# Attention products of a float32 kernel as 64 x 64 x 64 matmuls on the four quarters of the array, scores and outputs in one pair of PSUM banks

## The chip, the cores and the metric

The kernel runs on one core of a Trainium2 chip. A core has five engines with queues of their own: TensorE (PE in the profile; its weight loads are PEld), VectorE (DVE), ScalarE (ACT), GpSimd (POOL) and SyncE (SP, which here only issues transfers). The metric is the device time of one execution in microseconds (us).

## The reference

Chunked softmax attention, then two feed-forward layers, all in float32. Batch 8, 8 heads, 576 tokens, head size 64, chunks of 64 tokens; 4608 tokens in all, width 512, inner width 2048:

```python
scores = q_c @ k_c.T / sqrt(64)            # per batch, head and chunk: 64 x 64
attn = exp(scores - max(scores)); attn = attn / (sum(attn) + 1e-9)
x = attn @ v_c                             # 64 x 64, then heads side by side: [4608, 512]
h = x @ w_in1;  g = max(h, 0) + alpha * min(h, 0);  x = g @ w_out1
h = x @ w_in2;  out = (h - tanh(h)) @ w_out2
```

The layers' weights are float64 and are rounded to float32 on the chip.

## The kernel before

**The large products.** A layer runs over nine blocks of 512 tokens, layer 1 first and then layer 2. A block has 16 steps, one for each 128 inner features f: `up` (L414) makes `hps`, 128 features by 512 tokens, with 12 matmuls; `act_g` and `split_g` put it through the activation and split it into a high and a low part (`ghi`, `glo`); `down` (L472) adds it to the four accumulators `y` with 12 more matmuls, two steps later (`LAG`). Each of these 24 matmuls has 128 rows, 128 columns of weights and 512 moving columns.

**The attention beside it.** Tokens 0 to 511 (tiles 0 to 3, 128 tokens each, which are two chunks) have their attention worked out before the loop by functions with `_early` in their names. The 32 later tiles are worked out inside the blocks of layer 1, one block ahead of their use. A tile t goes through these stages, each put on a step of the plan by `at(step, ...)`, `s = base[t]` being its first:

- `att_a` (DVE transposes of 32 x 32 blocks) or `att_a_natural` (tiles 4 to 8 and three later ones: PE transposes `tr`, evicted by DVE and ACT) makes `qt` (queries, features on partitions) and `kbd`. In `kbd` the keys of the two heads of a pair stand block-diagonally, with zeros between, so that one matmul with 128 rows serves both heads.
- `att_s` (step s): 8 matmuls, one per head pair and chunk, 64 weight columns (`qt`) and 128 moving columns (`kbd`), into the bank `sc`.
- `att_e` (s+1) and `att_n` (s+2): maximum `mx`, difference, exponential `p`, sum `sm`, reciprocal `rd`, product on POOL.
- `att_t`, `att_d` (s+3): DVE transposes `p` into `pt`; four DVE and four ACT copies bring the 32 x 32 blocks into `ptb`, block-diagonal by chunk, zeros between.
- `att_v` (s+5): 8 matmuls, one per head, 64 weight columns (`v`) and 128 moving columns (`ptb`), into the bank `xp`.
- `att_x` (s+6): ACT and DVE split `xp` into `xh` and `xl`, which the next block's `up` reads.

Each of these matmuls is plain float32 and stands in the trace as two instructions. In steady state the tiles' first steps are four apart.

**What sets the order.** A scheduler orders each engine's instructions by the plan and by its own forecast of when operands are ready. An engine then takes its instructions in that order. While block 0 runs (to about 160 us), DVE, ACT and POOL also round the first layer's weights to float32 (`wm`, `w`; L107 to L154), and each `up` and `down` of that block waits for its own piece.

PSUM has eight banks: two for `hps`, four for `y`, one for `sc`, one for `xp`.

Of the kernel before, what the change touches and what calls it, by code (L numbers as in the profile page):

```python
# [18 lines left out]
# (h - tanh(h)) / h**3 = CC (s + CA) ((s + CB)**2 + CE), s = h*h, to float32 accuracy where |h| < 3/8  # L19
# [8 lines left out]
def kernel(  # L28
# [49 lines left out]
    kbd = const.tile([P, 2, HP, 2, 2, D], F32, name="kbd")  # L78
    ptb = const.tile([P, H, 2, D], F32, name="ptb")

# [157 lines left out]

    def att_a_natural(t):
        if t not in qts:  # L240
            new_qt([t, t + 1] if t in (4, 6) else [t])
        raw = raws.pop(t)
        for i in range(2):
            tr = ps_a.tile([P, HP, P], F32, tag=("sc", "xp")[i], name="tr")
            for hp in range(HP):
                nc.tensor.transpose(tr[:, hp, :], raw[i][:, hp * P:(hp + 1) * P], ident)
            if i == 0:
                nc.vector.tensor_copy(qts[t].rearrange("p h c d -> p h (c d)"), tr)
            else:
                for e in range(2):  # L250
                    r = slice(64 * e, 64 * e + 64)
                    nc.scalar.activation(
                        out=kbd[r, t % 2, :, :, e, :], in_=tr[r].rearrange("p h (c d) -> p h c d", c=2), func=AF.Copy
                    )
# [11 lines left out]
    def att_a(t):  # L266
        if t not in qts:
            new_qt((t, t + 1))
        raw = raws.pop(t)
        nc.vector.transpose(  # L270
            out=qts[t].rearrange("p h c d -> p h (c d)"), in_=raw[:, 0].rearrange("p h g i -> p h (g i)")
        )
        for e in range(2):
            r = slice(64 * e, 64 * e + 64)
# [5 lines left out]
    scs = {}  # L280

    def att_s(t, tag="sc"):
        qt = qts.pop(t)
        sc = ps_a.tile([P, HP, 2, D], F32, tag=tag, name="sc")
        for hp in range(HP):
            for c in range(2):
                nc.tensor.matmul(  # L287
                    out=sc[64 * c:64 * c + 64, hp],
                    lhsT=qt[:, hp, c, :],
                    rhs=kbd[:, t % 2, hp, c],  # L290
                    start=True,
                    stop=True,
                )
        scs[t] = sc

    def att_s_early(t):
        qt, kt = qts.pop(t), kts.pop(t)
        sc = ps_a.tile([P, HP, 2, D], F32, tag=("sc", "xp")[t % 2], name="sc")
# [13 lines left out]
    def att_e(t, early=False):  # L312
        scv = scs.pop(t).rearrange("p a e d -> p (a e) d")
        mx = stat.tile([P, H, 1], F32, tag="mx", name="mx")
        nc.vector.tensor_reduce(out=mx[:, :, 0], in_=scv, op=ALU.max, axis=AX.X)
        pool, tag = (stage, "st") if early else (att, "p")
        p = pool.tile([P, H, D], F32, tag=tag, name="p")
        nc.vector.tensor_tensor(out=p, in0=scv, in1=mx.to_broadcast([P, H, D]), op=ALU.subtract)
# [18 lines left out]
    def att_d(t):  # L337
        """Each 32 x 32 block goes to the partitions of its keys; the result is block-diagonal by chunk."""
        pt = pts.pop(t)
        for c in range(2):  # L340
            for a in range(2):
                o, i = 64 * c + 32 * a, 64 * c + 32 * (1 - a)
                nc.vector.tensor_copy(ptb[o:o + 32, :, c, 32 - 32 * a:64 - 32 * a], pt[i:i + 32, :, a, :])
                nc.scalar.activation(
                    out=ptb[o:o + 32, :, c, 32 * a:32 * a + 32], in_=pt[o:o + 32, :, a, :], func=AF.Copy
                )

    def att_v(t):
        vt = vts.pop(t)
        xp = ps_a.tile([P, HP, P], F32, tag="xp", name="xp")  # L350
        for hp in range(HP):
            for e in range(2):
                nc.tensor.matmul(  # L353
                    out=xp[64 * e:64 * e + 64, hp],
                    lhsT=vt[:, 2 * hp + e],
                    rhs=ptb[:, 2 * hp + e].rearrange("p c d -> p (c d)"),
                    start=True,
                    stop=True,
                )
# [27 lines left out]
    def x_parts(t, o):  # L387
        return ((xps[t], o, P),) if t >= NPT else ((xps[t][0], o, D), (xps[t][1], o + D, D))

    def att_xh(t, x, o):  # L390
        for xp, u, n in x_parts(t, o):
            nc.scalar.activation(out=x[0][:, :, u:u + n], in_=xp, func=AF.Copy)

    def att_xl(t, x, o):
        for xp, u, n in x_parts(t, o):
            nc.vector.tensor_tensor(  # L396
                out=x[1][:, :, u:u + n], in0=xp, in1=x[0][:, :, u:u + n].bitcast(F32), op=ALU.subtract
            )
# [48 lines left out]
    def tanhshrink(g, hp, n, f):  # L447
        """h - tanh(h); where |h| < 3/8 as h^3 times a cubic in h^2 that is the quotient to
        float32's accuracy, since the difference would cancel."""
# [7 lines left out]
        mask = kbd.bitcast(U32).rearrange("p u h c e d -> p (u h c e d)")[:, f % 2 * n:(f % 2 + 1) * n]  # L457
# [82 lines left out]
    turn = {4: 2, 5: 2, 6: 6, 7: 6, 8: 11}  # L540
    free = 0
    for unit in units:
# [15 lines left out]
        for t in unit:  # L558
            s = base[t]
            if t in turn:  # L560
                at(turn[t], att_a_natural, t)
# [35 lines left out]
    with tc.manual_schedule():  # L597
        make_identity(nc, ident)
        nc.vector.memset(zero, 0.0)
        nc.vector.memset(kbd, 0.0)  # L600
        nc.vector.memset(bias_sb, TS[1])
        nc.gpsimd.memset(ptb, 0.0)
# [171 lines left out]
```

## Time and profile before

| | |
|---|---|
| three runs | 1745.61, 1746.21, 1746.31 us; median 1746.21 |
| the profiled execution, first to last instruction | 1745.2 us |
| TensorE's mean granted clock there | 0.992 of full |
| busy: PE, DVE, ACT, POOL | 98%, 77%, 40%, 20% |
| layer 1 beyond block 0, 200 to 840 us | PE busy all 640 us, DVE 455 us |

Busy time is the union of an engine's instructions. Matmuls overlap in the pipeline, so that what a group of them costs is read from the distance between the starts of the groups around it, not from its own busy time.

### The profile page before, as it was taken

The page shows a single profiled execution, that of the slowest core. Times are in us where ns is not written, and L with a number is a line of the kernel's source. Part 1 is how long each engine was busy: PE and PEld are TensorE (multiplying, and loading weights), DVE is VectorE, ACT ScalarE, POOL GpSimd, SP SyncE. Part 2 cuts the span into 40 slices and gives each one's busy share as a digit, 9 for nine tenths or more (in the row PEclk, how much of TensorE's full clock was granted, in tenths as well). Part 3 has the DMA queues.
Part 4 walks back from the last instruction along what each step waited for, and adds up shares of the span by engine and source line. Part 5 has one row for each costly group of instructions (what it writes and reads, how often), then busy time and mean ns, then how long its engine had stood idle before and what let it go on. Part 6 is the DMA issues. An engine that isn't in the chain of part 4 may idle for free.

```text
span 1745.2 us, 22786 instructions
## 1 busy us (share of the span) xinstructions
PE 1704.2 (98%) x8365; PEld 1379.3 (79%) x8365; DVE 1344.3 (77%) x2188; ACT 694.5 (40%) x1312; POOL 345.4 (20%) x265
## 2 busy tenths in 40 slices
PE   8889999999999999999999999999999999999997
PEld 7667887888878888788888778788888888888885
DVE  8999857877677868675436787878788888888776
ACT  6665323323332324232334453434343434444433
POOL 2555000000000000000243222222222222222221
PEclk9999999999999999999999999999999999999999
DMA  9912306332252513320332010101010101000000
GB/s 248 259 50 55 109 14 144 80 101 75 76 113 42 152 31 127 61 79 7 127 91 73 1 48 1 48 1 49 1 48 1 49 1 49 1 25 1 24 1 25
DMA packets 215583, 108.45 MB, mean 62 GB/s; under 512 B 170912, under 2 KB 187312, under 8 KB 215472
## 3 DMA queue, kind: packets, MB, share of 16 engines
q1 hardware_dynamic: 215472, 107.01, 22.3%
q8 instruction: 65, 1.06, 0.3%
q14 instruction: 46, 0.38, 0.1%
HBM read 79.70 MB, written 27.26 MB: 61 GB/s over the span
## 4 chain that ended last, share of the span: by engine, by line
PE 61%; DVE 25%; ACT 8%; issue 5%; DMA 0%; SPq 0%; ACTq 0%; DVEq 0%
PE y L472 29%; PE hps L414 28%; DVE g L461 4%; DVE g L463 4%; DVE g L462 4%; DVE g L459 3%; ACT sq L454 2%; ACT ghi L444 2%; ACT w L456 2%; PE xp L353 2%; PE sc L287 2%; DVE kbd L458 2%; ACT th L455 1%; DVE xl L503 1%; DVE g L431 1%
## 5 line engine op out<-in xcount | busy, mean ns | idle before, releaser
L414 PE MATMUL hps<-xh,w 128*128 128x512 f32 (+1 forms) x2312 | 592.5, 396 | 11.5 <-ACT w L153 7.9
L414 PEld LDWEIGHTS hps<-xh,w 128*128 128x128 f32 x2312 | 430.2, 190 | 114.8 <-ACT w L153 8.8
L444 ACT ACTIVATE ghi<-g 128x512 fp32r<-128x512 f32 x288 | 181.9, 632 | 761.3 <-DVE g L463 450.1
L445 POOL TENSOR_TENSOR glo<-g,ghi 128x512 fp32r<-128x512 f32 x159 | 214.9, 1351 | 622.3 <-ACT ghi L444 580.2
L414 PE MATMUL hps<-xl,w 128*128 128x512 f32 (+1 forms) x1156 | 308.7, 389 | 0.0
L472 PE MATMUL y<-w,ghi 128*128 128x512 f32 x1152 | 294.0, 393 | 9.8 <-ACT ghi L444 5.2
L472 PE MATMUL y<-ghi,w 128*128 128x512 f32 x1152 | 292.3, 394 | 5.0 <-ACT ghi L444 2.5
L472 PEld LDWEIGHTS y<-w,ghi 128*128 128x128 f32 x1152 | 214.6, 188 | 62.4 <-ACT ghi L444 11.1
L472 PEld LDWEIGHTS y<-ghi,w 128*128 128x128 f32 x1152 | 217.3, 190 | 53.0 <-ACT ghi L444 3.5
L414 PEld LDWEIGHTS hps<-xl,w 128*128 128x128 f32 x1156 | 217.0, 188 | 45.3 <-DVE xl L396 0.3
L458 DVE TENSOR_SCALAR kbd<-sq 128x512 uint32<-128x512 f32 x144 | 136.5, 948 | 136.2 <-ACT sq L454 136.2
L435 DVE TENSOR_SCALAR g<-hps,alpha_sb 128x512 f32<-128x512 f32 x128 | 95.5, 746 | 113.6 <-PE hps L414 112.0
L329 POOL TENSOR_TENSOR p<-p,rd 128x512 f32<-128x512 f32 x35 | 38.2, 1091 | 632.2 <-DVE rd L328 554.6
L472 PE MATMUL y<-w,glo 128*128 128x512 f32 x576 | 159.6, 390 | 0.0
L472 PE MATMUL y<-glo,w 128*128 128x512 f32 x576 | 156.2, 390 | 0.0
L445 DVE TENSOR_TENSOR glo<-g,ghi 128x512 fp32r<-128x512 f32 x129 | 93.9, 728 | 63.7 <-ACT ghi L444 63.4
L472 PEld LDWEIGHTS y<-w,glo 128*128 128x128 f32 x576 | 108.4, 188 | 22.8
L463 DVE COPY_PREDICATED g<-kbd,th 128x512 f32<-128x512 uint32 x144 | 122.9, 853 | 4.4
L472 PEld LDWEIGHTS y<-glo,w 128*128 128x128 f32 x576 | 108.0, 188 | 22.6 <-issue 0.2
L461 DVE SCALAR_TENSOR_TENSOR g<-w,g 128x512 f32<-128x512 f32 x144 | 106.8, 741 | 0.0
L456 ACT ACTIVATE w<-sq,bias_sb 128x512 f32<-128x512 f32 x144 | 104.5, 726 | 0.0
L462 DVE SCALAR_TENSOR_TENSOR g<-sq,g 128x512 f32<-128x512 f32 x144 | 100.6, 698 | 4.7
(97 smaller groups left out, 1543.5 us busy)
## 6 DMA issues: line engine op xcount, KB each, us to landing
ysc<-yst SPq DMA_DIRECT2D x36, 256.0 KB, 2.7
yraw<-ysc SPq DMA_DIRECT2D x9, 1024.0 KB, 5.6
out_dram<-yst SPq DMA_DIRECT2D x36, 256.0 KB, 2.4
w<-in_moe_w_in_dram SPq DMA_DIRECT2D x16, 512.0 KB, 6.5
w<-in_moe_w_out_dram SPq DMA_DIRECT2D x16, 512.0 KB, 6.1
rw<-in_moe_w_in_dram SPq DMA_DIRECT2D x32, 256.0 KB, 2.9
rw<-in_moe_w_out_dram SPq DMA_DIRECT2D x32, 256.0 KB, 3.3
w<-wm SPq DMA_DIRECT2D x32, 256.0 KB, 2.1
```

Source lines behind the costliest of these rows:

```text
L329: engine.tensor_tensor(out=p, in0=p, in1=rd.to_broadcast([P, H, D]), op=ALU.mult)
L414: nc.tensor.matmul(out=hp[:, cols], lhsT=w[:, a, m], rhs=x[b][:, kk, cols], start=(kk == 0 and i == 0), stop=(kk == KD - 1 and i == 2),)
L435: nc.vector.tensor_scalar(out=g, in0=hp, scalar1=0.0, scalar2=alpha_sb[:, f:f + 1], op0=ALU.min, op1=ALU.mult)
L444: nc.scalar.activation(out=hi, in_=g, func=AF.Copy)
L445: lo_engine.tensor_tensor(out=lo, in0=g, in1=hi.bitcast(F32), op=ALU.subtract)
L456: nc.scalar.activation(out=w, in_=sq, func=AF.Square, bias=bias_sb)
L458: nc.vector.tensor_scalar(out=mask, in0=sq, scalar1=0.375 ** 2, scalar2=None, op0=ALU.is_ge)
L459: nc.vector.scalar_tensor_tensor(out=g, in0=sq, scalar=cc, in1=hp, op0=ALU.mult, op1=ALU.mult)
L461: nc.vector.scalar_tensor_tensor(out=g, in0=w, scalar=ce, in1=g, op0=ALU.add, op1=ALU.mult)
L462: nc.vector.scalar_tensor_tensor(out=g, in0=sq, scalar=ca, in1=g, op0=ALU.add, op1=ALU.mult)
L463: nc.vector.copy_predicated(g, mask, th)
L472: nc.tensor.matmul(out=acc[t], lhsT=lhsT, rhs=rhs, start=(f == 0 and i == 0), stop=(f == KF - 1 and i == 2))
```

## The change

The two attention products of the 32 later tiles are cut to 64 rows by 64 columns: one matmul for each head and chunk, 16 for each product of a tile in place of 8, with 64 moving columns in place of 128. Row half e (scores) or c (outputs) of the array writes bank e or c of a pair of banks, so that each matmul has one quarter of the array. `kbd` becomes `ktc`, without zeros and half as large; `ptb` loses its zeros too; the two memsets that wrote the zeros are gone. Keys are then transposed by one DVE instruction in place of two, and evicted by one ACT instruction in place of two for the tiles with PE transposes.

The banks `sc` and `xp` become one tile of two banks with one buffer (`new_banks`). The scores take the first 256 columns of both banks; the outputs of the tile that is due in the same step (`beside`) take the last 256. `att_v` moves from step s+5 to s+4, where the next tile's `att_s` stands, and behind it. `att_a_natural` writes both banks as well, and the early scores take the same pair (`first_banks`). Tile 8's transposes move from step 11 to step 10.

```diff
-    kbd = const.tile([P, 2, HP, 2, 2, D], F32, name="kbd")
-    ptb = const.tile([P, H, 2, D], F32, name="ptb")
+    ktc = const.tile([P, 2, HP, 2, D], F32, name="ktc")
+    ptb = const.tile([P, 2, HP, 2, 32], F32, name="ptb")
...
+    def new_banks(name):
+        return ps_a.tile([P, 2, 512], F32, tag="a", name=name)
...  att_a
-        for e in range(2):
-            r = slice(64 * e, 64 * e + 64)
+        for i, to in enumerate((qts[t], ktc[:, t % 2])):
             nc.vector.transpose(
-                out=kbd[r, t % 2, :, :, e, :],
-                in_=raw[r, 1].rearrange("p h (c b) i -> p h c (b i)", c=2),
+                out=to.rearrange("p h c d -> p h (c d)"), in_=raw[:, i].rearrange("p h g i -> p h (g i)")
             )
...  att_s
-        sc = ps_a.tile([P, HP, 2, D], F32, tag=tag, name="sc")
+        banks[t] = new_banks("sc")
+        sc = banks[t][:, :, 0:HP * D].rearrange("p e (h d) -> p e h d", h=HP)
         for hp in range(HP):
             for c in range(2):
-                nc.tensor.matmul(
-                    out=sc[64 * c:64 * c + 64, hp],
-                    lhsT=qt[:, hp, c, :],
-                    rhs=kbd[:, t % 2, hp, c],
+                for e in range(2):
+                    r = slice(64 * e, 64 * e + 64)
+                    nc.tensor.matmul(
+                        out=sc[64 * c:64 * c + 64, e, hp, :],
+                        lhsT=qt[r, hp, c, :],
+                        rhs=kt[r, hp, c, :],
...  att_v
-        xp = ps_a.tile([P, HP, P], F32, tag="xp", name="xp")
+        both = banks.get(beside.get(t)) or new_banks("xp")
+        xp = both[:, :, HP * D:].rearrange("p c (h d) -> p c h d", h=HP)
         for hp in range(HP):
             for e in range(2):
-                nc.tensor.matmul(
-                    out=xp[64 * e:64 * e + 64, hp],
-                    lhsT=vt[:, 2 * hp + e],
-                    rhs=ptb[:, 2 * hp + e].rearrange("p c d -> p (c d)"),
+                for c in range(2):
+                    r = slice(64 * c, 64 * c + 64)
+                    nc.tensor.matmul(
+                        out=xp[64 * e:64 * e + 64, c, hp, :],
+                        lhsT=vt[r, 2 * hp + e],
+                        rhs=ptb[r, e, hp].rearrange("p a i -> p (a i)"),
...  the plan
-            pv = s + 5
-            at(pv - 2, load_v, t)
-            at(pv, att_v, t, first=True)
-            at(pv + 1, lambda t: att_x(t, get_x(t // NPT), t % NPT * P), t)
+    for t in range(NPT, NT // P):
+        pv = base[t] + (5 if t == 7 else 4)
+        if t != 7:
+            beside[t] = next((u for u in base if base[u] == pv), None)
+        at(pv - 2, load_v, t)
+        at(pv, att_v, t)
+        at(pv + 1, lambda t: att_x(t, get_x(t // NPT), t % NPT * P), t)
```

PE in a block of layer 1 beyond block 0, at the scores of one tile, before:

```order
L472 MATMUL y_1842<-glo,w_10_1366 128x512
L472 MATMUL y_1843<-glo,w_10_1366 128x512
L287 MATMUL sc<-kbd,qt 64x128 x8
L414 MATMUL hps<-xh,w_13_1448 128x512 x8
L414 MATMUL hps<-xl,w_13_1448 128x512 x4
L472 MATMUL y_1840<-ghi,w_11_1451 128x512
```

The same place now:

```order
L478 MATMUL y_1912<-glo,w_10_1411 128x512
L478 MATMUL y_1913<-glo,w_10_1411 128x512
L287 MATMUL sc<-ktc,qt 64x64 x16
L358 MATMUL sc<-ptb,v 64x64 x16
L420 MATMUL hps<-xh,w_13_1494 128x512 x8
L420 MATMUL hps<-xl,w_13_1494 128x512 x4
L478 MATMUL y_1910<-ghi,w_11_1497 128x512
```

Before, the outputs of the tile before (`xp`, L353) stand 24 large matmuls further on, alone as well; now they stand right behind the scores, in the same tile of banks, and so carry its name `sc`. Beyond block 0 there are 27 such pairs and one output product alone at the end; five of the score products are cut in two by large matmuls, as were five products before.

PE at the end of block 0, before (tiles 7 and 9):

```order
L472 MATMUL y_641<-glo,w_12_1545 128x512
L353 MATMUL xp<-ptb,v 64x128 x8
L287 MATMUL sc<-kbd,qt 64x128 x8
L414 MATMUL hps<-xh,w_15_1605 128x512 x4
L414 MATMUL hps<-xh,w_0_385 128x512 x8
```

And now (transposes of tile 8, outputs of tile 6, scores of tile 8, outputs of tile 7):

```order
L478 MATMUL y_634<-glo,w_12_1592 128x512
L251 MATMUL tr<-ident,w_15_525 128x128 x8
L358 MATMUL xp<-ptb,v 64x64 x16
L287 MATMUL sc<-ktc,qt 64x64 x16
L420 MATMUL hps<-xh,w_15_1650 128x512 x8
L420 MATMUL hps<-xl,w_15_1650 128x512 x4
L358 MATMUL xp<-ptb,v 64x64 x16
```

The four attention groups around step 13 each take the one pair of banks in turn, so that each waits until the one before it has been read. The scores of tiles 6 and 7 come some 100 large matmuls later than before; on DVE, conversions of the weights stand ahead of these tiles' steps.

DVE at that place now (tiles 6 and 7, from the sum over tile 6's `p`):

```order
L328 TENSOR_REDUCE sm<-p 128x8
L404 TENSOR_TENSOR xl<-sc,xh 128x2x4x64
L330 TENSOR_SCALAR sm<-sm 128x8
L331 RECIPROCAL rd<-sm 128x8
L337 STREAM_TRANSPOSE pt<-p 128x512
L272 STREAM_TRANSPOSE ktc<-raw 128x512
L346 COPY ptb<-pt 32x8x32 x4
L316 TENSOR_REDUCE mx<-sc 128x8
L319 TENSOR_TENSOR p<-sc,mx 128x512
L328 TENSOR_REDUCE sm<-p 128x8
L404 TENSOR_TENSOR xl<-sc,xh 128x2x4x64
```

Before, conversions (`wm`) stood between these steps of a tile:

```order
L325 TENSOR_REDUCE sm<-p 128x8
L128 ISA wm<-wm,wr 128x1024
L122 TENSOR_SCALAR wm<-wm 128x512
L124 SCALAR_TENSOR_TENSOR wm<-w_13_766,wm 128x512
L327 TENSOR_SCALAR sm<-sm 128x8
L124 SCALAR_TENSOR_TENSOR wm<-w_14_572,wm 128x512
L431 SCALAR_TENSOR_TENSOR g<-neg,nalpha_sb,g 128x512
L128 ISA wm<-wm,wr 128x1024
L328 RECIPROCAL rd<-sm 128x8
```

Now two tiles' chains follow each other with nothing of another kind between their steps but one transpose of keys.

## Rows read from the trace of the kernel before

**Rows 1.** The page: busy us (share of the span) and count

```profile
PE 1704.2 (98%) x8365; PEld 1379.3 (79%) x8365; DVE 1344.3 (77%) x2188; ACT 694.5 (40%) x1312; POOL 345.4 (20%) x265
```

**Rows 2.** Windows: length; PE, PEld, DVE, ACT, POOL busy (count); clock; DMA, GB/s

```profile
30.00:155.00 125.00, 103.69 (x537) 79.25 (x537) 123.72 (x180) 87.50 (x164) 66.17 (x45) 0.93 0.55 148
...
200.00:840.00 640.00, 640.00 (x3362) 515.48 (x3361) 455.20 (x904) 190.86 (x394) 27.65 (x26) 1.00 0.30 76
840.00:1745.00 905.00, 890.22 (x3886) 726.17 (x3884) 701.30 (x974) 380.37 (x683) 234.17 (x175) 1.00 0.09 32
```

**Rows 3.** Waits of PE from 30 to 160 us: total, times, longest

```profile
PE hps L414 <- ACT w L153: 7.9, 2, 4.6
```

**Rows 4.** Timeline of PE in layer 1: start, length, instructions

```profile
308.80 1.98 PE L414 MATMUL hps<-xh,w 128*128 128x512 f32 x8
310.61 1.07 PE L414 MATMUL hps<-xl,w 128*128 128x512 f32 x4
...
313.33 1.07 PE L472 MATMUL y<-glo,w 128*128 128x512 f32 x4
314.33 1.09 PE L287 MATMUL sc<-kbd,qt 128*64 128x128 f32 x16
315.36 2.11 PE L414 MATMUL hps<-xh,w 128*128 128x512 f32 x8
317.30 1.07 PE L414 MATMUL hps<-xl,w 128*128 128x512 f32 x4
...
338.58 1.09 PE L287 MATMUL sc<-kbd,qt 128*64 128x128 f32 x16
```

**Rows 5.** Windows of line 287 (scores) alone, 155 to 840 us

```profile
155.00:840.00 685.00, 30.15 (x416) 22.91 (x416) 1.00 0.31 79
```

**Rows 6.** Windows of line 353 (outputs) alone, 155 to 840 us

```profile
155.00:840.00 685.00, 31.07 (x448) 24.06 (x448) 1.00 0.31 79
```

**Rows 7.** Timeline of PE before the loop: early tiles, 64 x 64 matmuls

```profile
16.88 1.15 PE L303 MATMUL sc<-kt,w 64*64 64x64 f32 x32
...
18.77 0.82 PE L378 MATMUL xpe<-pte,v 64*64 64x64 f32 x32
...
21.27 0.69 PE L378 MATMUL xpe<-pte,v 64*64 64x64 f32 x32
21.89 0.71 PE L639 MATMUL more<-zero 128*128 128x128 f32 x4
23.79 1.02 PE L378 MATMUL xpe<-pte,w 64*64 64x64 f32 x32 [1.19 <-DVE xl L396]
```

**Rows 8.** Line 353, 312 to 322 us: weight loads and PE's sequencer, first start

```profile
L353 PEld LDWEIGHTS xp<-ptb,v x16: 133/137/137, 321.0 to 321.7; 128*64 128x64 f32 x16
...
L353 PEldq EVENT_SEMAPHORE  x1: 51/51/51, 316.9 to 316.9; - x1
```

**Rows 9.** Timeline of all engines in layer 1, the tile of 314.33

```profile
326.00 1.04 POOL L329 TENSOR_TENSOR p<-p,rd 128x512 f32<-128x512 f32 x1 [25.30 <-DVE rd L328]
...
327.08 0.71 DVE L334 STREAM_TRANSPOSE pt<-p 128x512 f32<-128x512 f32 x1 [0.67 <-POOL p L329]
...
327.82 1.70 ACT L344 ACTIVATE ptb<-pt 32x256 f32<-32x256 f32 x4 [2.32 <-DVE pt L334]
```

**Rows 10.** Groups by line and form: count, busy, mean ns

```profile
L275 DVE STREAM_TRANSPOSE kbd<-raw 64x512 f32<-64x512 f32 x48 | 32.8, 691 | 7.4 <-DMA raw<-in_k_dram 6.9
...
L319 ACT ACTIVATE p<-p 128x512 f32<-128x512 f32 x36 | 22.7, 631 | 95.1 <-DVE p L318 95.1
...
L378 PE MATMUL xpe<-pte,v 64*64 64x64 f32 x64 | 1.5, 225 | 0.0
```

**Rows 11.** Timeline of PE at the end of block 0

```profile
155.05 5.64 PE L414 MATMUL hps<-xh,w 128*128 128x512 f32 x16 [3.35 <-ACT w L153]
...
162.34 1.07 PE L414 MATMUL hps<-xl,w 128*128 128x512 f32 x4
```

**Rows 12.** Timeline of DVE there: tile 7's low part

```profile
160.92 0.68 DVE L396 TENSOR_TENSOR xl<-xp,xh 128x512 fp32r<-128x512 f32 x1
```

More of the change, by code (lines that the diff above doesn't have):

```diff
@@ L242, in att_a_natural @@
         raw = raws.pop(t)
+        both = new_banks("tr")
         for i in range(2):
-            tr = ps_a.tile([P, HP, P], F32, tag=("sc", "xp")[i], name="tr")
+            tr = both[:, i].rearrange("p (h t) -> p h t", h=HP)
             for hp in range(HP):
@@ L269, in att_a, with att_s @@
         raw = raws.pop(t)
[L270 to L274, printed above, removed]
+        for i, to in enumerate((qts[t], ktc[:, t % 2])):
             nc.vector.transpose(
-                out=kbd[r, t % 2, :, :, e, :],
-                in_=raw[r, 1].rearrange("p h (c b) i -> p h c (b i)", c=2),
-            )
-    scs = {}
-    def att_s(t, tag="sc"):
-        qt = qts.pop(t)
-        sc = ps_a.tile([P, HP, 2, D], F32, tag=tag, name="sc")
+                out=to.rearrange("p h c d -> p h (c d)"), in_=raw[:, i].rearrange("p h g i -> p h (g i)")
+            )
+    scs, banks, beside = {}, {}, {}
+    def att_s(t):
+        qt, kt = qts.pop(t), ktc[:, t % 2]
+        banks[t] = new_banks("sc")
+        sc = banks[t][:, :, 0:HP * D].rearrange("p e (h d) -> p e h d", h=HP)
         for hp in range(HP):
             for c in range(2):
-                nc.tensor.matmul(
-                    out=sc[64 * c:64 * c + 64, hp],
-                    lhsT=qt[:, hp, c, :],
-                    rhs=kbd[:, t % 2, hp, c],
-                    start=True,
-                    stop=True,
-                )
+                for e in range(2):
[4 more added lines that the diff above has]
+                        rhs=kt[r, hp, c, :],
+                        start=True,
+                        stop=True,
+                    )
         scs[t] = sc
@@ L297, in att_s_early @@
         qt, kt = qts.pop(t), kts.pop(t)
-        sc = ps_a.tile([P, HP, 2, D], F32, tag=("sc", "xp")[t % 2], name="sc")
+        sc = first_banks[:, t % 2].rearrange("p (h c d) -> p h c d", h=HP, c=2)
         for hp in range(HP):
@@ L312, in att_e @@
     def att_e(t, early=False):
-        scv = scs.pop(t).rearrange("p a e d -> p (a e) d")
-        mx = stat.tile([P, H, 1], F32, tag="mx", name="mx")
-        nc.vector.tensor_reduce(out=mx[:, :, 0], in_=scv, op=ALU.max, axis=AX.X)
+        scv = scs.pop(t)
+        a, b = (HP, 2) if early else (2, HP)
+        mx = stat.tile([P, a, b, 1], F32, tag="mx", name="mx")
+        nc.vector.tensor_reduce(out=mx[:, :, :, 0], in_=scv, op=ALU.max, axis=AX.X)
         pool, tag = (stage, "st") if early else (att, "p")
         p = pool.tile([P, H, D], F32, tag=tag, name="p")
-        nc.vector.tensor_tensor(out=p, in0=scv, in1=mx.to_broadcast([P, H, D]), op=ALU.subtract)
+        nc.vector.tensor_tensor(
+            out=p.rearrange("p (a b) d -> p a b d", a=a), in0=scv, in1=mx.to_broadcast([P, a, b, D]), op=ALU.subtract
+        )
         nc.scalar.activation(out=p, in_=p, func=AF.Exp, scale=scale)
@@ L337, in att_d @@
     def att_d(t):
-        pt = pts.pop(t)
+        pt, pn = pts.pop(t), ptb.rearrange("p e h a i -> p (e h) a i")
         for c in range(2):
@@ L385, in att_v_early, with x_parts @@
         xps[t] = xp
-    def x_parts(t, o):
-        return ((xps[t], o, P),) if t >= NPT else ((xps[t][0], o, D), (xps[t][1], o + D, D))
+    def x_parts(t, x, o):
+        if t >= NPT:
+            return ((xps[t], x[:, :, o:o + P].rearrange("p h (c d) -> p c h d", c=2)),)
+        return tuple((xps[t][c], x[:, :, o + c * D:o + (c + 1) * D]) for c in range(2))
     def att_xh(t, x, o):
-        for xp, u, n in x_parts(t, o):
-            nc.scalar.activation(out=x[0][:, :, u:u + n], in_=xp, func=AF.Copy)
+        for xp, to in x_parts(t, x[0], o):
+            nc.scalar.activation(out=to, in_=xp, func=AF.Copy)
     def att_xl(t, x, o):
[L395 to L398, printed above, removed]
+        for (xp, hi), (_, to) in zip(x_parts(t, x[0], o), x_parts(t, x[1], o)):
+            nc.vector.tensor_tensor(out=to, in0=xp, in1=hi.bitcast(F32), op=ALU.subtract)
         xps.pop(t)
@@ L641 @@
         dummy = ps_y.tile([P, P], F32, tag="y3", name="dummy")
+        first_banks = new_banks("first")
         x0 = get_x(0)
@@ L684 @@
         att_xl(0, x0, 0)
-        more = ps_a.tile([P, P], F32, tag="sc", name="more")
+        more = first_banks[:, 0, 0:P]
         warm(2, more)
@@ L698 @@
         att_x(3, x0, 3 * P)
-        at_ps = ps_a.tile([P, KF], F32, tag="sc", name="at_ps")
+        at_ps = first_banks[:, 0, 0:KF]
         nc.tensor.transpose(at_ps, arow[:KF, :P], ident[:KF, :KF])
```

26 lines of the change are left out of this document (10 added, 16 removed).

## The prediction

> **What bounds the kernel now.** I read the page first, then the windows by stretch, then PE's waits, then PE's timeline around one attention product. The page has PE busy for 98% of the span [rows 1]. The windows say where that share is a bound [rows 2]. From 200 to 840 us, layer 1 beyond block 0, PE is busy in all 640 us at full clock, and DVE in 455: there the end moves by what PE is spared and by nothing else. From 30 to 155 us it is the other way round: DVE is busy in 123.7 of 125 us and PE in 103.7, and PE's largest waits are for weights that DVE and ACT round (7.9 us in two) [rows 3]. Layer 2, from 840 us, has no attention; the change alters only the tile in which its mask lies.
>
> **What one attention product costs now.** Eight large matmuls start 1.81 us apart from the next group (308.80 to 310.61), 0.227 us each, so twelve take 2.72 us. Between 313.33 and 317.30 stand four, then the scores, then eight: 3.97 us [rows 4]. The scores therefore cost 3.97 - 2.72 = 1.25 us, of which 1.03 lie between their first start and that of the next large matmul; the other 0.22 is lost at the two edges. From 155 us on there are 416 / 16 = 26 score products and 448 / 16 = 28 output products [rows 5, 6], 54 x 1.25 = 67.5 us.
>
> **What one will cost.** The form on all four quarters exists already in the trace: the early tiles' output products, 32 instructions of 64 x 64 with 64 moving columns, each row half with a bank of its own. One instruction lasts 0.22 us [rows 10]. The group at 21.27 us lasts 0.69, so its starts are (0.69 - 0.22) / 31 = 15 ns apart, and the next large matmul starts 0.62 after its first. The group at 18.77 lasts 0.82: 19 ns. The early scores, which use two quarters only, last 1.15: 30 ns [rows 7]. A quarter thus takes one instruction in some 60 ns, and four work side by side.
> A pair is 64 instructions: 0.62 + 32 x 0.015 = 1.10 us, and with the 0.22 of the edges, paid once, 1.32. By the group of 19 ns it would be 0.13 more for each half, 1.58. I take 1.38, near the 15 ns: in the steady state the sequencer runs ahead, since it dealt with the wait of the outputs of 321.0 at 316.9 us [rows 8], with 17 large matmuls still to start. So some 17 instructions of a pair stand ready when it begins, and the rest are issued while these run. Whether issue keeps up for 64 in a row no row shows; that is the doubt in this term.
> Now 27 pairs and one output product alone (0.22 + 0.62 = 0.84): 27 x 1.38 + 0.84 = 38.1 us. The five products that are cut in two cost the same edges as the five before. The term is 67.5 - 38.1 = **29.4 us gained**; its ends are 31.0 (pairs of 1.32) and 24.0 (1.58).
> The Trainium skill (TensorEngine Tiling (Array Packing), Performance Considerations, Instruction Overhead) speaks against this step: a matmul carries some 60 cycles of overhead on trn2, and a tiling factor is not to be taken from a dimension that is already small, which here are the 64 moving columns. At 2.4 GHz that is 25 ns an instruction (an estimate from that page), a pair of 0.22 + 0.15 + 1.60 = 1.97 us and a time near 1733. The trace does not agree for 32 instructions: 15 ns.
>
> **Are the operands there a step earlier?** The outputs of a tile move to the step of the next tile's scores, 338.58 for the tile of 314.33. Its last copies into `ptb` end at 327.82 + 1.70 = 329.5 [rows 4, 9]: 9 us in hand. The values `v` are still asked for two steps ahead. Behind a waiting pair would stand all large matmuls, so that margin matters. The one pair of banks is free again once the last pair's scores and outputs are read; in the new order both lie ahead of the tile's product on POOL, which began at 326.00 [rows 9], 12 us after the scores. Pairs come 24 us apart. So I cost both at nothing; without the 9 us the outputs' wait would fall on PE in full. What comes later for the outputs (`xh` behind the difference of the scores in the same banks) is wanted only by the next block.
>
> **DVE, ACT and the memsets.** The second half of each key transpose goes: 691 ns for each of 24 tiles [rows 10], 17 us of DVE, all in a stretch where DVE has 29% to spare, save 1.4 us in block 0. The two memsets end before the first transposed tile arrives. The smaller ACT evictions lie beside PE work. Nothing of this moves the end.
>
> **Block 0.** PE gains nothing there while DVE is the bound. The new order has the weights' conversions ahead of the attention of tiles 6 and 7, and then their steps one behind the other with no other work between. Up to tile 7's low part `xl`, which block 1's last four `up` matmuls wait for, DVE has about as much work as before (some 0.6 us less). But for each of two tiles it now stands through the exponential (0.63) [rows 10] and POOL's product (1.04) [rows 9], 3.3 us, and I add 1.7 for the hand-overs of the one pair of banks (transposes of tile 8, outputs of 6, scores of 8, outputs of 7, each after the last one's readers): 5.0. So that `xl`, done at 161.6 before [rows 12], comes 4.4 us later. By then PE has 20 more large matmuls behind it than at 162.34 before [rows 11], 4.5 us, and tile 9's scores (0.95) still ahead, since these are counted in the pairs. Then the pair of tiles 9 and 8 follows 12 matmuls on and waits, by my reckoning 1.5 us, for tile 8's steps. Net 4.4 - 4.5 - 0.95 + 1.5 = **0.5 us lost**. No row shows such an order, so the bounds are wide: 4 gained (nothing of the 5.0 appears) to 6 lost (the waits add up and the early matmuls are themselves late).
>
> **Sum.** 1745.2 - 29.4 + 0.5 = 1716.3; the median of the runs stands 1.0 above the profiled span, so 1717.
>
> **Rivals.**
> Issue bound. The sequencer feeds the quarters no faster than in the slowest early group, 1.02 us or 26 ns [rows 7], that is a pair of 0.22 + 0.15 + 64 x 0.026 = 2.03 and a gain of 67.5 - 54.8 - 1.2 = 11.5: time 1735. For it: 64 in a row is twice what the trace has. Against it: that group had an empty queue and a wait behind it.
> Block 0 takes back. The chains of tiles 6 to 8 cost PE 6 to 12 us instead of 0.5, because every group there needs the same two banks: 1722 to 1729, say 1726. For it: DVE has 1.3 us of slack in 125. Against it: the weights come earlier, and they are what PE waited for.
> Two quarters only. If scores and outputs overlap no better than the early scores, 30 ns: pair 2.29, gain 4.3, time 1743. Against it: those used the two diagonal quarters alone; the new ones use all four, as the groups at 15 and 19 ns do.
> Slower. The quarters do not overlap in the loop, and 64 instructions go one by one at a quarter's own 60 ns: a pair of 0.37 + 3.84 = 4.21 against 2.50, 27 x 1.71 and 1.0 for the last product: 47 us lost, 1794. It decides from a spacing of (2.50 - 0.37) / 64 = 33 ns on. Against it stand three early groups at 15 to 26 ns; for it only that none of them ran behind large matmuls of the other number format.
> The Trainium skill (TensorE: Matmul & The Clock Gate, Part 1, "Wait — 56ns, not 53.3ns?") has a rule that would end there: about 62 ns of sequencer time per matmul where hardware decoding is off, by which a pair would be 4.3 us and the time about 1798. The early groups at 15 ns do not agree with it.
> The change does not do what it says: the pairs' outputs wait in the loop after all (for `ptb`, `v` or the banks), 1 us or more each, and eat the gain: 1745. The 9 us in hand speak against it.
>
> **How the numbers follow.** Forecast 0.68, 1710 to 1728; issue bound 0.13; block 0 takes back 0.11; two quarters 0.02; waits in the pairs 0.02; one by one 0.04. The range for 8 in 10 leaves the last three out and cuts into the issue-bound case: **1710 to 1734**. A measurement of this kernel tells 0.2% (3.5 us) from no change. Faster by more: 0.68 + 0.13 + 0.11 = 0.92; within 0.2%, where 1743 and 1745 lie: 0.02 + 0.02 = 0.04; slower: 0.04.
>
> **What would show it.** In layer 1 of the new timeline: scores and outputs of 32 instructions each back to back, the next large matmul 1.10 to 1.20 us after the first score, and 23.1 us from pair to pair in place of 24.25 (24.25 - 1.12). PE stays busy throughout at clock 1.00. A spacing that grows within a pair from about the fortieth instruction on would be the issue rate. In block 0: PE waits at tile 8's transposes and at the scores and outputs behind them, and block 1's first `xl` matmuls start near 167 us. The forecast is wrong if a pair costs over 2 us, if PE waits at the outputs of a pair, or if block 1 begins more than 6 us later than I have it.

## The result, and the profile after

The changed kernel takes 1730.22 us (median of four runs, 1729.36 to 1731.79) against 1746.01 for the kernel before beside it: a ratio of 0.9906, 95% interval 0.9892 to 0.992. That is faster by 0.9%, inside the range, and 13 us slower than the forecast of 1717. The profiled execution lasts 1727.6 us, 17.6 less than that of before.

Where the time went is read by counting: the matmuls of `up` and `down` are the same in both kernels, so the start of the n-th one tells how far the work is. "Block 1's start" below is the 393rd, the first on a low part `xl` in block 1 of the changed kernel; the "end of the attention" is the 3101st, past the last attention product in every kernel here.

| | before | after | gained |
|---|---|---|---|
| block 1's start | 167.7 | 172.0 | -4.3 |
| from there to the end of the attention | 686.1 | 666.4 | 19.7 |
| the rest, layer 2 in the main | 891.5 | 889.1 | 2.3 |

The middle stretch holds 2708 large matmuls, 614.1 us at 0.2268 each in both kernels. What is left is 72.0 us before and 52.3 after. Of the 52.3, 9.4 are waits of PE, and what follows from them, that before did not have; without them attention costs 42.9, and the change would have gained 29.1 there.

The windows of after, in the order of [rows 2] (length; PE, PEld, DVE, ACT, POOL busy; clock; DMA, GB/s):

```profile
30.00:155.00 125.00, 98.21 (x604) 75.95 (x604) 113.24 (x163) 77.50 (x147) 72.13 (x44) 0.89 0.53 147
200.00:840.00 640.00, 633.72 (x4265) 516.87 (x4264) 456.57 (x912) 193.55 (x402) 28.50 (x26) 1.00 0.31 79
```

Two things are new. From 200 to 840 us PE is no longer busy throughout. And in block 0 DVE, which was busy in all but 1.3 of 125 us, now stands for 11.8.

PE's timeline around one pair answers to [rows 4]:

```profile
196.14 1.07 PE L478 MATMUL y<-glo,w 128*128 128x512 f32 x4
197.13 0.69 PE L287 MATMUL sc<-ktc,qt 64*64 64x64 f32 x32
197.65 0.65 PE L358 MATMUL sc<-ptb,v 64*64 64x64 f32 x32
198.23 2.11 PE L420 MATMUL hps<-xh,w 128*128 128x512 f32 x8
```

The next large matmul starts 1.10 us after the first score. The 32 scores take 0.52 us, 16 ns from start to start; the outputs last 0.65, of which the last one alone is 0.22, so that their starts are (0.65 - 0.22) / 31 = 14 ns apart. That is 15 ns over the pair, and it does not grow. Counted over all whole pairs, such a pair delays the large matmuls by 1.18 + 0.11 at the edge behind it, 1.29 us; a product of before costs 1.12 + 0.11 = 1.23.

PE's waits beyond block 0 (total, times, longest) are in one row, and two stretches of PE's timeline show what it means:

```profile
PE hps L420 <- DVE g L444: 6.2, 6, 2.9
```

```profile
327.22 1.07 PE L478 MATMUL y<-glo,w 128*128 128x512 f32 x4
331.21 2.77 PE L420 MATMUL hps<-xh,w 128*128 128x512 f32 x8 [2.92 <-DVE g L444]
333.77 1.91 PE L420 MATMUL hps<-xl,w 128*128 128x512 f32 x4
335.48 2.19 PE L478 MATMUL y<-ghi,w 128*128 128x512 f32 x8
...
525.12 0.33 PE L287 MATMUL sc<-ktc,qt 64*64 64x64 f32 x2
526.90 1.43 PE L420 MATMUL hps<-xh,w 128*128 128x512 f32 x5 [1.45 <-DVE g L444]
```

`up` needs a bank of `hps` that DVE frees with the second instruction of `g`. After the stand of 2.92 us five large matmuls still run at the higher clock; then the granted clock is 0.50 (332.6 to 335.8 us), its lower level, and eight take 0.43 us each in place of 0.227: 1.6 us more. The 9.4 us are in the main that row's waits, this lower clock, and 1.0 at the pair of tiles 9 and 8.

DVE's timeline ahead of the first stand, the longest, shows what it had in front of that `g`:

```profile
323.37 0.29 DVE L118 TENSOR_SCALAR wm<-wm 128x256 f32<-128x256 f32 x1 [0.35 <-ACT wm L107]
...
325.93 1.29 DVE L272 STREAM_TRANSPOSE qt<-raw 128x512 f32<-128x512 f32 x2
327.15 0.67 DVE L272 STREAM_TRANSPOSE ktc<-raw 128x512 f32<-128x512 f32 x1
327.74 0.65 DVE L316 TENSOR_REDUCE mx<-sc 128x8 f32<-128x512 f32 x1
328.43 0.69 DVE L319 TENSOR_TENSOR p<-sc,mx 128x512 f32<-128x512 f32 x1
329.04 0.74 DVE L441 TENSOR_SCALAR g<-hps,alpha_sb 128x512 f32<-128x512 f32 x1
...
330.48 0.68 DVE L444 SCALAR_TENSOR_TENSOR g<-hps,g 128x512 f32<-128x512 f32 x1
```

It stands for nothing there: from 323.4 us on it goes from one instruction to the next for 7.8 us, through conversions, three transposes, the maximum and the difference, and `g` comes behind them. Ahead of the second:

```profile
512.36 0.16 DVE L330 TENSOR_SCALAR sm<-sm 128x8 f32<-128x8 f32 x1
517.89 0.71 DVE L272 STREAM_TRANSPOSE ktc<-raw 128x512 f32<-128x512 f32 x1 [5.38 <-DMA raw<-in_k_dram]
518.53 0.25 DVE L118 TENSOR_SCALAR wm<-wm 128x256 f32<-128x256 f32 x1
518.70 0.68 DVE L444 SCALAR_TENSOR_TENSOR g<-hps,g 128x512 f32<-128x512 f32 x1
...
526.16 0.68 DVE L444 SCALAR_TENSOR_TENSOR g<-hps,g 128x512 f32<-128x512 f32 x1
```

It stood 5.4 us at a key transpose whose loads had not landed, with a `g` two places behind. That `g` delayed PE by 0.22 us only:

```profile
519.43 2.12 PE L420 MATMUL hps<-xh,w 128*128 128x512 f32 x8 [0.22 <-DVE g L444]
```

The wait of 1.45 us was ended by the next step's `g`, at 526.16; between the two DVE stood 0.86 us for a conversion and for the rest ran conversions, a transpose and copies. So a late load lies in front of this wait, but not directly.

Block 0, PE's timeline at its end; it answers to [rows 11]:

```profile
142.74 1.07 PE L478 MATMUL y<-glo,w 128*128 128x512 f32 x4
147.36 0.63 PE L251 MATMUL tr<-ident,w 128*128 128x128 f32 x4 [3.55 <-issue]
148.78 1.11 PE L251 MATMUL tr<-ident,w 128*128 128x128 f32 x4 [0.79 <-DVE qt L253]
150.58 1.13 PE L358 MATMUL xp<-ptb,v 64*64 64x64 f32 x32 [0.69 <-ACT ktc L255]
154.97 1.13 PE L287 MATMUL sc<-ktc,qt 64*64 64x64 f32 x32 [3.27 <-DVE xl L404]
158.69 3.53 PE L420 MATMUL hps<-xh,w 128*128 128x512 f32 x8 [2.59 <-ACT w L153]
...
163.70 0.69 PE L358 MATMUL xp<-ptb,v 64*64 64x64 f32 x32 [0.55 <-PE hps L420]
...
172.03 1.07 PE L420 MATMUL hps<-xl,w 128*128 128x512 f32 x4
```

Four groups stand behind each other, each waiting until the readers of the one before have left the pair of banks; 8.3 us of waits in the first four rows that have one. For the first of these the profile names no releaser ("issue"); it ends 0.1 us after DVE's last reading of the pair before, which is

```profile
146.58 0.68 DVE L404 TENSOR_TENSOR xl<-sc,xh 128x512 fp32r<-128x512 f32 x1
```

### The profile page after: what moved, and what is told of

It reads as the page before. It is cut to its first block, busy times and chain, and to the rows that moved or that the text cites. A ratio compares the mean times of both kernels' runs of the same rounds, so it can differ in the third digit from the quotient of the medians.

```text
span 1727.6 us, 24773 instructions
## 1 busy us (share of the span) xinstructions
PE 1670.8 (97%) x9389; PEld 1360.8 (79%) x9389; DVE 1324.7 (77%) x2163; ACT 689.5 (40%) x1304; POOL 352.3 (20%) x264
## 4 chain that ended last, share of the span: by engine, by line
PE 51%; DVE 21%; ACT 8%; issue 5%; SPq 3%; DMA 3%; POOL 0%; ACTq 0%; DVEq 0%; POOLq 0%
PE y L478 25%; PE hps L420 24%; DVE g L467 4%; DVE g L469 4%; DVE g L468 4%; DVE g L465 3%; SPq L232 3%; ACT ghi L450 2%; ACT sq L460 2%; DVE ktc L464 2%; ACT w L462 2%; DMA rw<-in_moe_w_in_dram 1%; DVE xl L509 1%; ACT th L461 1%; PE sc L287 1%
## 5 line engine op out<-in xcount | busy, mean ns | idle before, releaser
L464 DVE TENSOR_SCALAR ktc<-sq 128x512 uint32<-128x512 f32 x144 | 136.3, 947 | 135.0 <-ACT sq L460 135.0
L478 PEld LDWEIGHTS y<-glo,w 128*128 128x128 f32 x576 | 108.4, 189 | 23.1 <-POOL glo L451 0.6
L469 DVE COPY_PREDICATED g<-ktc,th 128x512 f32<-128x512 uint32 x144 | 122.9, 853 | 4.4
```

What stands on the lines that cost most here:

```text
L464: nc.vector.tensor_scalar(out=mask, in0=sq, scalar1=0.375 ** 2, scalar2=None, op0=ALU.is_ge)
L469: nc.vector.copy_predicated(g, mask, th)
L478: nc.tensor.matmul(out=acc[t], lhsT=lhsT, rhs=rhs, start=(f == 0 and i == 0), stop=(f == KF - 1 and i == 2))
```

## Experiments

Two questions were open: what took 4 us in block 0, and what makes PE wait beyond it. The first theory for both was the pair of banks, which is one tile with one buffer. All medians are of four or five runs, each ratio against the kernel before on the same chip.

**1. The old products on the new plan.** The kernel before, with its products of 128 rows; `sc` and `xp` become halves of the pair, and steps are those of the change.

```
+    sc = banks[t][:, 0].rearrange("p (h c d) -> p h c d", h=HP, c=2)
+    both = banks.get(beside.get(t)) or new_banks("xp");  xp = both[:, 1]...
+    pv = base[t] + (5 if t == 7 else 4)
```

> The kernel before, with its products of 128 rows and block-diagonal operands kept, but with the new plan: sc and xp one tile of two banks with one buffer, the outputs at step s+4 behind the next tile's scores, PE transposes into the same pair. Theory: the plan alone saves one edge of 0.11 us for each of 27 pairs (3 us) and costs what the changed kernel lost elsewhere: about 4 us in block 0 and 9 us of waits in layer 1; 1746 - 3 + 4 + 9 = 1756 (1752 to 1760), and the quarters alone are then worth some 26 us. Rival: the losses belong to the new form of the products (more instructions, other tiles), not to the plan; then this is 1743 to 1746.

1756.95 us, ratio 1.0061 (1.0048 to 1.0074): slower than before. Block 1 starts at 178.6. The quarters alone are worth 26.7 us on this plan. That the time came out as expected is luck. The expectation put 9 us of waits into layer 1; there it was wrong: beyond 240 us this kernel waits for 0.6 us in all. A pair of the old products saves 0.36 us in place of 0.11, and block 1 starts 10.9 us later than before, not 4.

```profile
PE hps L420 <- DVE g L444: 0.6, 2, 0.4
```

**2. The same steps, banks of their own.** As 1, with `sc` and `xp` as before.

```
+    pv = base[t] + (5 if t == 7 else 4)      # outputs behind the next tile's scores
-    sc, xp: one tile of two banks            # two tiles of one bank, as before
```

> The kernel before, with its outputs moved to step s+4 behind the next tile's scores and tile 8's transposes at step 10, but sc and xp banks of their own as before. The old products on the whole new plan started block 1's first low-part matmul at 178.6 (before: 167.7). Theory: of these 10.9 us the one pair of banks is the greater part; here it starts at 167 to 171, and 1750 (1746 to 1753) with the waits in layer 1. Rival: the moved steps alone, with tile 8's, cost block 0 as much: 176 to 180 and 1755 to 1759.

1740.46 us, ratio 0.9962 (0.9949 to 0.9974), faster than expected, and faster than before. Between 1 and 2 nothing differs but the tile of the banks: 16.5 us. It falls in block 0 and right behind it: the 701st large matmul starts at 265.8 in the first and at 247.3 in the second; from there to the end of the attention both take 600 us. The windows from 30 to 165 us of before, of 2, of 1 and of the changed kernel say through which engine:

```profile
30.00:165.00 135.00, 113.65 (x573) 87.21 (x574) 133.68 (x194) 92.23 (x173) 73.02 (x50) 0.92 0.55 143
```

```profile
30.00:165.00 135.00, 114.62 (x576) 86.67 (x576) 134.12 (x192) 91.83 (x172) 74.34 (x50) 0.92 0.56 144
```

```profile
30.00:165.00 135.00, 102.01 (x505) 78.68 (x506) 124.19 (x175) 87.20 (x164) 67.34 (x46) 0.90 0.49 135
```

```profile
30.00:165.00 135.00, 105.07 (x679) 81.12 (x680) 122.96 (x179) 86.29 (x162) 76.44 (x47) 0.87 0.50 137
```

DVE is the third busy figure: idle for 1.3 and 0.9 us with two banks of their own, for 10.8 and 12.0 with the one pair. DVE is what bounds block 0, so its idle time is the loss: 9.9 us more in 1 than in 2, whose block 1 starts 10.0 us earlier. In PE's timeline of 1 the longest wait for the banks is that of tile 8's scores for tile 6's low part:

```profile
152.99 1.98 PE L359 MATMUL xp<-ptb,v 128*64 128x128 f32 x16 [1.28 <-ACT kbd L256]
162.72 1.98 PE L292 MATMUL sc<-kbd,qt 128*64 128x128 f32 x16 [7.76 <-DVE xl L402]
```

**3. to 6. Fewer or other turns of the pair in block 0.** A turn is one use of the pair, from the first write to the last reading. If each turn costs PE a wait for its readers, one turn fewer must help.

```
3:  base of tile 8: 12 -> 11 (its scores beside tile 6's outputs, at 11; its own outputs stay at 16)
4:  outputs of tile 6: step 11 -> 12, behind tile 8's scores
5:  turn = {..., 8: 10} -> {..., 8: 11}
6:  low part a step later (as 9 below), and for all tiles with PE transposes, 4 to 8 too,
    both halves' transposes ahead of their copies
```

> The changed kernel, with tile 8's scores a step earlier (11 in place of 12), so that they share one turn of the pair of banks with tile 6's outputs: one turn fewer in block 0. Theory: each turn of the one pair costs PE a wait for the readers of the turn before it; the 3.3 us that tile 8's scores wait for tile 6's low part go, block 1 begins some 3 us earlier, 1730.2 becomes 1727 (1725 to 1728.5). Rival: DVE's conversions of the weights set the end of block 0, and the turns only show where PE waits meanwhile; the time stays within 1 us, 1729 to 1731.

In this kernel tile 7's outputs are made from tile 8's probabilities, which are copied ahead of them; what is issued is as much. 1736.94 us, ratio 0.9947 (0.9934 to 0.996); block 1 starts at 180.5.

> The changed kernel, with tile 6's outputs at step 12 behind tile 8's scores in place of step 11: one turn of the pair of banks fewer in block 0, the order of the probabilities kept. Theory: each turn costs PE the readers of the turn before; the waits of 0.69 at tile 6's outputs and 3.27 at tile 8's scores become one, block 1's first low-part matmul starts at 169 (168 to 170.5) in place of 172.0, and 1730.2 becomes 1727 (1725 to 1728.5). Rival: the conversions of the weights on DVE set the end of block 0; 171 to 173, 1729 to 1731.

1734.54 us, 0.9936 (0.9923 to 0.9948); 178.0.

> The changed kernel, with tile 8's transposes back at step 11 as before the change, which puts them behind tile 6's outputs. Theory: as many turns of the pair of banks as before, each held as long, so block 1 starts within 2 us of 172 and the time is 1728 to 1732. Rival: tile 8's chain is what ends block 0, and transposes, copies, scores one behind the other make it 3 us longer: 174 to 177, 1732 to 1736.

1735.03 us, 0.9942 (0.9928 to 0.9955); 180.0.

> As the last, but with the halves together for tiles 4 to 8 too, so that block 0 changes: each of these tiles then holds the pair of banks for one group of 8 transposes in place of two groups of 4 with 14 to 18 large matmuls between. Theory: the time for which a group holds the one pair of banks is what block 0 pays; block 1's first low-part matmul starts at 167 to 170 in place of 172.0, and the time is 1717 (1714 to 1721). Rival: block 0 ends when DVE has done the conversions; the start stays within 1 us of 172 and the time that of the kernel with the later halves and the low part alone.

1733.45 us, 0.9926 (0.9913 to 0.9938); 175.9, with a wait of 7.4 us at scores for a low part.

All four miss their theory, and only 5 has its rival's time, though not its start: no turn taken away helped, and every rearrangement cost 4 to 8.5 us at block 1's start. In 4 the wait of tile 8's scores for tile 6's low part did go, and one for a weight came in its place; PE's largest wait from 120 to 190 us there:

```profile
PE hps L420 <- ACT w L153: 11.2, 1, 11.2
```

So the price of a turn is not additive. That it depends on what DVE has in its queue there, since the weights' conversions move with the turns, fits these rows and is not shown. That the one buffer costs block 0 is shown by 1 and 2, with the old products; which order would cost least is not.

**7. The outputs apart from the scores.** Quarters as in the change, but from tile 9 on the outputs stand two steps behind the next tile's scores.

```
-    pv = base[t] + (5 if t == 7 else 4)
+    pv = base[t] + (5 if t == 7 else 4 if t < 9 else 6)
```

> The changed kernel, with the outputs of tiles 9 and later two steps behind the next tile's scores (s+6), in a turn of the banks of their own: quarters, but no pairs. Theory: a product by itself costs 0.72 + 0.11 = 0.83 us, two of them 1.66 against 1.29 for a pair; 23 pairs less cost 8.5 us, 1739 (1736 to 1742) if the other waits of layer 1 stay as they are. Rival: what a pair shares is nothing (the second product costs the same wherever it stands): 1729 to 1732. If the low part's move out of the step of the next tile's maximum also takes DVE's lateness away, the time lies lower by up to 8 us and PE's waits at hps are gone.

1731.89 us, 0.9918 (0.9905 to 0.9931): 1.7 above the change, which is no clear difference, where the products alone should have cost 8.5. PE's timeline gives the price that was expected, 0.63 from the outputs to the next large matmul, and each delays these by 0.72 + 0.11:

```profile
209.01 1.07 PE L478 MATMUL y<-glo,w 128*128 128x512 f32 x4
210.01 0.69 PE L358 MATMUL xp<-ptb,v 64*64 64x64 f32 x32
210.64 2.11 PE L420 MATMUL hps<-xh,w 128*128 128x512 f32 x8
```

The product term is right; what is missing is in the waits. This kernel has the halves of the PE transposes apart and the one pair of banks too, and waits 1.2 us for `g` where the changed one waits 6.2.

**8. The halves together.** Only for the three later tiles with PE transposes: in the changed kernel both halves are one tile, the keys' transposes wait for the copy of the queries, and the order puts them 24 large matmuls later. The edit, then PE's timeline of after and of this kernel:

```
-        for i in range(2):      # transposes of half i, then its copy
+        for i in range(2):      # transposes of both halves
+        for i in range(2):      # then the two copies            (tiles above 8)
```

```profile
261.45 0.60 PE L251 MATMUL tr<-ident,rawn 128*128 128x128 f32 x4
...
267.16 0.60 PE L251 MATMUL tr<-ident,rawn 128*128 128x128 f32 x4
```

```profile
261.15 1.03 PE L252 MATMUL tr<-ident,rawn 128*128 128x128 f32 x8
```

> The changed kernel, but for the three later tiles with PE transposes the four transposes of the keys stand right behind those of the queries, before either copy. Theory: in the changed kernel both halves are one tile of banks, so the keys' transposes wait for the copy of the queries; the scheduler therefore puts them 24 large matmuls later (261.45 and 267.16 us), the raw buffer comes free some 6 us later, the loads of the next two tiles start 8 us later than before, DVE stands up to 5.4 us at the key transposes, and PE at hps. With the halves together the waits of PE at hps beyond block 0 (6.2 us, and 2.5 us of half-speed clock and edges behind them) go: 8 us, from 1730.2 to 1722 (1719 to 1725). Rival: DVE is late because maximum, difference and low part now fall in one step; then the waits stay and the time is 1729 to 1732.

1725.54 us, 0.9876 (0.986 to 0.9892): 4.7 less than the change (2.6 in the profiled executions), the lowest median of all, though its interval still touches that of the change. The stretch from block 1's start to the end of the attention falls from 666.4 to 663.3 us. PE's waits for `g` fall only to 4.4, none longer than 1.6:

```profile
PE hps L421 <- DVE g L445: 4.4, 6, 1.6
```

With none of 2.9 us the clock stays up: 1.00 in the window from 300 to 350 us, where the changed kernel has 0.97. The theory was half right. DVE stands at tile transposes for loads as long as in the changed kernel (20 us in all beyond 250 us in both), so the loads' start is not what the edit improved.

**9. and 10. The low part a step later**, in the changed kernel, and with the halves together.

```
-        at(pv + 1, att_x ...)
+        at(pv + (1 if t < 8 else 2), att_x ...)
```

> The changed kernel, with xh and xl of tiles 8 and later two steps behind the outputs in place of one, so that the low part no longer falls in the step of the next tile's maximum and difference. Theory: that step is what makes DVE late with g (the kernel with the outputs apart has the split transposes too, and no wait at hps); PE's waits at hps beyond block 0 fall from 6.2 us to under 1.5, 1730.2 becomes 1723 (1721 to 1726). Rival: with the outputs apart DVE only had 8.5 us more of PE work to catch up in; then the waits stay here, 1728 to 1731.

1728.61 us, 0.9906 (0.9892 to 0.9921): the same as the change. The waits stay, 6.2 us in six:

```profile
PE hps L420 <- DVE g L444: 6.2, 6, 2.5
```

> Both edits: the later PE-transposed tiles' halves together, and the low part a step later. Theory: two causes of the same lateness, which add up: no wait at hps is left beyond block 0, the stretch from block 1's first low-part matmul to the end of the attention takes about 657 us (614.1 of large matmuls, 36 of attention, 5 of edges, 2 of transposes) against 666.4; 1720 (1718 to 1723). Rival: the two edits take away the same waits, and the time is that of the better one alone, about 1725.

1726.66 us, 0.9879 (0.9864 to 0.9894): the same as 8. Beside the maximum or not, the low part is no cause.

**11. The later PE transposes a step earlier**, with the halves together, so that the 64 loads behind them start earlier.

```
-            turn[t] = base[t] - 1
+            turn[t] = base[t] - 2
```

> The changed kernel with the later PE-transposed tiles' halves together, as in the kernel of that name, and with these transposes two steps ahead of the tile's scores in place of one. Theory: behind each such tile 64 loads stand in a train that takes SP 36 to 41 us whatever PE does (before: 259.8 to 300.3; now 267.8 to 308.6), while a step of PE has become shorter; DVE reaches the key transposes before the loads, stands there with g queued behind, and PE waits at hps. With the train a step (5.8 us) earlier DVE stands under 10 us at the tile transposes beyond 250 us (23 with the halves together alone), PE's waits at hps fall from 4.4 us to under 1, and 1725.5 becomes 1720.5 (1718 to 1722.5). Rival: the waits come from the order of DVE's work at the faster pace, and the loads only show there; 1724 to 1727.

1726.3 us, 0.989 (0.9876 to 0.9903): the same as 8, as the rival had it. The train starts at 256.8 in place of 262.2 and ends at 298.7 in place of 303.7, but DVE still stands 17 us for loads (20 in 8), and PE waits 4.9.

**12. Fewer conversions a step**, with the halves together.

```
-        s = KF + 5 + 3 * i
+        s = KF + 5 + 7 * i // 2
```

> The changed kernel with the later PE-transposed tiles' halves together (1725.5), and the second layer's weights loaded and converted at 3.5 steps a piece in place of 3, over steps 21 to 133 in place of 21 to 118. Theory: a step of PE is 5.8 us now and was 6.06, while SP's loads and DVE's and ACT's side work per step are as many; conversions whose loads are late in SP's train hold up ACT and DVE with g behind them. A seventh less of them per step lets PE's waits at hps beyond block 0 fall from 4.4 us (5.4 with the one at a cut score product) to 2 or less: 1722 (1720 to 1724). Rival: the waits stand behind the key transposes of the tiles that follow a PE-transposed one, whatever the conversions do; 1724.5 to 1727.

1728.24 us, 0.9891 (0.9874 to 0.9907): no better than 8, against the theory, and above the rival's bounds. PE waits 4.5 us in sum; one wait is of 2.6 us, and the clock falls behind it as in the changed kernel:

```profile
312.02 2.60 PE L421 MATMUL hps<-xh,w 128*128 128x512 f32 x8 [2.58 <-DVE g L445]
314.42 1.91 PE L421 MATMUL hps<-xl,w 128*128 128x512 f32 x4
```

Read together, the runs fit a matter of pace. A tile's four steps hold 96 large matmuls, 21.77 us, and its two products:

| kernel | us a tile | PE's waits for `g` beyond 240 us |
|---|---|---|
| before | 21.77 + 2.46 = 24.2 | 0 |
| 1, one pair of banks, halves apart | 21.77 + 2.10 = 23.9 | 0.6 |
| 2, banks of their own | 21.77 + 2.10 = 23.9 | 0 |
| 7, one pair, halves apart | 21.77 + 1.66 = 23.4 | 1.2 |
| the change, one pair, halves apart | 21.77 + 1.29 = 23.1 | 6.2 |
| 8, one pair, halves together | 23.1 | 4.4 |

Between 1 and the change steps, banks and split halves are alike; the products are not. The new form spares PE 0.8 us a tile and brings the waits. The work beside PE has to be done in the same, shorter step, and at 23.1 us a tile it no longer always is. No run changed the pace alone, so this reading is argued, not shown. DVE's stands for loads do not explain the column by themselves: beyond 250 us they are 14 us before, 20 in the change, and 21 in 7, where PE waits 1.2.

## Why the prediction was right, and where it was not

The direction, the range and the mechanism of the gain were right; the forecast of 1717 was 13 us too low. By its own terms, in the profiled executions:

| term | forecast | measured |
|---|---|---|
| products from block 1 on | 29.4 gained | 29.1 gained |
| waits in layer 1 beyond block 0 | 0 | 9.4 lost |
| block 0 | 0.5 lost | 4.3 lost |
| the rest | 0 | 2.3 gained |
| sum | 28.9 | 17.7 (17.6 by the spans) |

**What one product costs and will cost: right.** 1.25 was 1.23, and a pair of 1.38 was 1.29; the two errors point opposite ways and partly cancel, which is luck. The spacing was read from early groups of 32 instructions at 15 ns, and 64 in a row behind large matmuls start 15 ns apart as well; what was added to the 1.32 in case they would not did not come. The issue-bound rival (26 ns), the two-quarters rival (30) and the one-by-one rival (60) are out: the spacing does not grow within a pair. Of the sign named for the pairs (1.10 to 1.20 us to the next large matmul) the lower end came. The rule that was weighed against it, some 60 cycles of overhead for each matmul (the Trainium skill, TensorEngine Tiling (Array Packing), Instruction Overhead), would have made that 1.10 about 1.75 (an estimate from that page: 64 x 25 ns and the 0.15 of a tail); the trace does not agree.

**Are the operands there a step earlier: right.** In layer 1 PE waits at no pair but that of tiles 9 and 8, at its outputs, for `ptb` (1.0 us; 1.5 was forecast).

**"DVE has 29% to spare ... nothing of this moves the end": this step failed,** and with it "PE stays busy throughout at clock 1.00". It priced DVE's slack from an average over 640 us at the old pace. In the profile of before DVE already stood 14 us for loads at the tile transposes; that cost PE nothing. DVE's waits there, 200 to 840 us:

```profile
DVE qt L270 <- DMA raw<-in_q_dram: 7.5, 3, 2.6
DVE kbd L275 <- DMA raw<-in_k_dram: 6.9, 3, 2.5
```

At 23.1 us a tile PE waits for `g`, six times in 600 us, and the longest wait is followed by the lower clock. The sum forgot that a step which becomes shorter takes slack from everything that is done once a step. Experiment 8 gives back a part (PE's waits fall from 6.2 to 4.4 us). That the low part's place, the start of the loads' train or the rate of the conversions would be the cause is refuted as far as 9 to 12 go. Which of DVE, ACT and SP's loads is the one that must become shorter stays open.

**Block 0: the right place, the wrong size.** PE waits where the text said: at tile 8's transposes and at the scores and outputs behind them. The step that failed is the 5.0 us: DVE ends tile 7's low part at 169.9, 8.3 us later than at 161.6 before, where 4.4 was taken:

```profile
169.26 0.68 DVE L404 TENSOR_TENSOR xl<-xp,xh 128x512 fp32r<-128x512 f32 x1
```

The path behind it was not right either. PE does not wait for this low part: it comes to block 1's first low-part matmul 2.1 us after it is done, with no gap in front. What makes PE late are its waits ahead of that, 31.2 us in all from 30 us on against 21.2 before, and the clock, granted 0.88 from 30 to 172 us against 0.93 from 30 to 168 before. Block 1's start came at 172.0 in place of 167. That lies within the bound of 6 lost, and below the 6 to 12 of the rival "block 0 takes back". Experiments 1 and 2 show a cause, the one buffer of the pair; with the old products it costs 16.5 us, which is nearly three times what the plan's steps gain (5.6). How much of it the quarters pay no run shows, since none has them on banks of their own. By the Trainium skill (PSUM — Partial Sum Buffer, PSUM bank collisions raise a hardware error) different row tiles are not able to access one bank at the same time; so the two halves of a product are to keep to a bank each, and the pair can't simply be divided between scores and outputs. No run here tried it.

**The rest.** Layer 2 became 2.3 us shorter in this execution. Among the kernels run here, whose layer 2 is alike, that part lies between 888.3 and 891.5 us; it is not explained, and not put down to the change.

## What to carry to other kernels

When an edit shortens the engine that bounds a stage, look up what else is done once per step, and compare its waits with the new length of the step, not with its average share: here slack that was free at the old pace was the first thing to be used up. Merging two buffers into one tile couples all their readers, also where only halves are meant; here its price was paid where another engine is the bound, so it is to be worked out there. And a schedule around such a buffer is sensitive: four plausible shifts cost 4 to 8.5 us each at block 1's start.

## What the runs showed of the hardware

64 float32 matmul instructions of 64 x 64 x 64 in a row, on four quarters of the array, start 15 ns apart on the mean (16 among the scores, 14 among the outputs), also directly behind large matmuls of another number format. Stands of 2.6 us (experiment 12) and 2.9 us were each followed by five large matmuls at the higher clock and then some eight at the lower (0.43 us each against 0.227). A stand of 1.9 us in experiment 1 was so too (211.36 us); after the waits of experiment 8, up to 1.6 us, the clock stayed at its higher level.
